# More row tiles in seven-product form, and a new layout of the last stage, in a Fourier-mixing and gated-FFN kernel

## The chip, the cores and the metric

The kernel runs on one core of one Trainium2 chip. The metric is the device time of one execution in microseconds; the times of several executions are given as a median. The profile comes from one execution of its own.

## The reference

The input `A_x` is one sequence of 2048 rows of 448 values. It is normalised row by row; from the result come a Fourier mix `s` and a gate `g`, and the output is `x + s * g`. (`B_x` isn't used.)

```python
def _A_ref(x, dft_seq_re, dft_seq_im, dft_hid_re, dft_hid_im):
    a = jnp.einsum("bsd,ed->bse", x, dft_hid_re)
    b = jnp.einsum("bsd,ed->bse", x, dft_hid_im)
    y = jnp.einsum("ts,bse->bte", dft_seq_re, a) - jnp.einsum("ts,bse->bte", dft_seq_im, b)
    return y

def _B_ref(x, w_gate, w_up, w_down):
    return (_gelu(x @ w_gate) * (x @ w_up)) @ w_down

x = A_x
xn = _layernorm(x, axis=-1)
s = _A_ref(xn, A_dft_seq_re, A_dft_seq_im, A_dft_hid_re, A_dft_hid_im)
g = _silu(_B_ref(xn, B_w_gate, B_w_up, B_w_down))
return x + s * g
```

Everything is fp32; `F` is 1792. The sequence matrices are 2048 x 2048 each.

## The kernel before

**Numbers.** TensorE works on `float32r` values. Each fp32 value is split into a high part (a rounded copy, by ACT) and a low part (the difference, by DVE), and a product is the sum of high x high, high x low and low x high, accumulated in one PSUM bank.

**Order.** All instructions stand in the order in which the program is written (`manual_schedule`, L418); each engine runs its own in that order and waits by semaphore for what it needs. SP's queue issues nearly all transfers, also in order; POOL's issues those that accumulate. A transfer on either queue carries one of eight semaphores in turn, and so also waits for the transfer eight places earlier.

**Stages.**

1. Load x, normalise, transpose, and the first feed-forward group (L419 to L615). The gate's 14 column tiles of `F` are taken in seven groups of two (`GROUPS`).
2. The other six groups (L643 to L732). Each has four blocks; a block is one call of `strassen` (L359), the gate and up products of one `F` tile for half of the rows, in a seven-product form, with four steps of the down projection (`down_one`, L318) of earlier blocks between them. `prep_s` (L231) makes sums of the next weight tiles on POOL and splits them; `load_w` and `load_d` bring them, into two halves of `raw`. Beside this, `sum_copy` and `sum_add` (L621 to L629) make sums of blocks of the sequence matrices in DRAM: a DRAM-to-DRAM copy on SP, and then a transfer on POOL's queue that adds to it. They make `sums`, 5 slots of 512 columns for each of eight passes.
3. The hidden transform (L743, `hid_mm`), for 16 row tiles k of the sequence: 22 matmuls of 448 columns each, into two of four PSUM banks. The outcome is either stored plainly, in high and low parts (`hid_plain`), or, for ten k, as seven combinations of column halves, split (`hid_seven`): a tile `TS[k]` of 128 x 3136. Six k are plain (`KP`). Of the ten, six stay in SBUF (`KR`); the four in `KX` share two tiles: all are written to DRAM (`td`) and two at a time are loaded back.
4. The last stage (L996): eight passes j, each for two row tiles t of the output (2j and 2j + 1). Per pass, each of the ten k takes seven products, `seven` (L942): 7 pairs of matmuls, high x (high, low), 448 columns, and low x high, 224 columns. That is the 2 x 2 product (two t, by the real and the imaginary part) times (real and imaginary, by two halves of the columns), in seven products for eight. The six plain k take 72 matmuls of 448 columns, `plain` (L953). Weights come from `ct` and `sums` in pieces of two k (`load_c`), get their last two sums on DVE (`combine_c`, L845), and are split (`prep_c`, L864) three units before PE uses them; a pass has 13 units. Seven PSUM banks hold the products and `gather` (L965) combines them; `give` (L980) adds the plain part and the other half, multiplies by g, adds x and stores. Two `TS` tiles are exchanged per pass, each in one transfer of 1568 KB on SP.

```python
nc.tensor.matmul(ps[q][:, :D], a, v, start=first, stop=False, skip_group_check=True)
nc.tensor.matmul(
    ps[q][:, :HD], b, v[:, :HD], start=False, stop=last, skip_group_check=True
)
```

Of the kernel before, what the change touches and what calls it, by code (L numbers as in the profile page):

```python
# [8 lines left out]
F32 = mybir.dt.float32  # L9
# [4 lines left out]
P = 128  # L14
# [16 lines left out]
KR = (0, 2, 4, 6, 9, 12)  # L31
KX = ((5, 8), (11, 14))
KP = (1, 3, 7, 10, 13, 15)
F_AT = {0: 0, 2: 0, 4: 1, 5: 0, 6: 1, 8: 0, 9: 1, 11: 0, 12: 1, 14: 1}

WHERE = "BAC"
UNITS = 13
DRAIN = {12: 2, 2: 2}


def order(j):


    q = [(t, k) for t in range(2) for k in KP]
    q = [q[i : i + 4] for i in range(0, 12, 4)]
    first = [KX[(j + 1) % 2], q[0]]
    return first[:: 1 if j else -1] + [KR[0:2], KR[2:4], KR[4:6], KX[j % 2], q[1], q[2]]

NS = 5


def slot_of(j, n):

    seven = [isinstance(what, tuple) for what in order(j)]
    return (0 if seven[n] else NS) + sum(s == seven[n] for s in seven[:n]), seven[n]
# [4 lines left out]
def fnet_geglu(ctx: ExitStack, tc: tile.TileContext, x, ct, et, wgu, wd, out):  # L62
# [20 lines left out]
    ps_mm = ctx.enter_context(tc.tile_pool(name="ps_mm", bufs=4, space=bass.MemoryType.PSUM))  # L83
    ps_tp = ctx.enter_context(tc.tile_pool(name="ps_tp", bufs=2, space=bass.MemoryType.PSUM))
    ps_o = ctx.enter_context(tc.tile_pool(name="ps_o", bufs=1, space=bass.MemoryType.PSUM))
# [6 lines left out]
    a_w = [sb.tile([P, 2560], FR, name=f"w{i}", tag=f"w{i}") for i in range(3)]  # L92
    a_d = [sb.tile([P, 1792], FR, name=f"wd{i}", tag=f"d{i}") for i in range(2)]
    a_r = sb.tile([P, 2 * 1536], F32, name="raw")
    a_t = sb.tile([P, 8 * 512], F32, name="tmp", tag="tmp")
# [16 lines left out]
    turns = [0]  # L112

    def o_tile(name, which=None):

        turns[0] += 1
        tag = which or "AB"[turns[0] % 2]
        return ps_o.tile([P, 512], F32, name=name, tag=tag)
# [44 lines left out]
    def turn_mm(c, k):  # L163
        pt = ps_tp.tile([P, 4, P], F32, name=f"pt{c}_{k}", tag="tp")
# [115 lines left out]
    def gu_ps(f, c):  # L280
        names = [f"gu{f}_{c}_{g}" for g in range(2)]
        if (f, c) == (0, 1):
            return [o_tile(n) for n in names]
        return [ps_mm.tile([P, 512], F32, name=n, tag="mm") for n in names]


    hs_of = {}

    def hs_tile(name, dt=FR):
        return sb.tile([P, 2, 512], dt, name=name, tag="hs", bufs=6)  # L290

    def new_hs(f, c):
        hs_of[f, c] = hs_tile(f"hs{f}_{c}")
        return hs_of[f, c]
# [3 lines left out]
    def act(f, c, pg):  # L298
        acts[0] += 1
        gt = tmp(acts[0] % 2)  # L300
# [17 lines left out]
    def down_one(gi, c, wdn, kk):  # L318
        if gi > 0 and kk >= 2:
            po = ps_tp.tile([P, 512], F32, name=f"po{gi}_{c}_{kk}", tag="tp")  # L320
        else:
            po = o_tile(f"po{gi}_{c}_{kk}")
# [36 lines left out]
    def strassen(f, p, w, late, dn, preps):  # L359
# [7 lines left out]
        def bank(i):  # L367
            return ps_mm.tile([P, 512], F32, name=f"x{i}_{f}_{p}", tag="mm")
# [19 lines left out]
        dn[1]()  # L388
        preps()
# [28 lines left out]
    with tc.manual_schedule():  # L418
# [11 lines left out]
        junk = hs_tile("junk")[:, 0]  # L430
# [124 lines left out]
        xf[2] = hs_tile("xf2", F32)  # L555
# [23 lines left out]
        for c in (2, 3):  # L579
# [6 lines left out]
            if c == 2:  # L586
                xf[3] = hs_tile("xf3", F32)
# [16 lines left out]
            if c == 2:  # L604
                nws[0] = prep_s(2, s_raw, nc.vector)
            else:
                nwdn = prep_d(GROUPS[1], draw)
                late_split = combine(1)
# [10 lines left out]
        sums = [dram.tile([P, NS, 512], F32, name=f"sums{j}") for j in range(NK // 2)]  # L619

        def sum_copy(j):  # L621
            src = ct[j, :NS].rearrange("n p c -> p n c")
            for q in range(2):
                nc.sync.dma_start(sums[j][:, :, 256 * q : 256 * (q + 1)], src[:, :, :256])

        def sum_add(j):
            src = ct[j, :NS].rearrange("n p c -> p n c")
            for n in (slice(0, 2), slice(2, NS)):
                nc.gpsimd.dma_start(sums[j][:, n], src[:, n, 256:768], accum_op=ALU.add)  # L629
# [13 lines left out]
        for gi in range(1, len(GROUPS)):  # L643
# [3 lines left out]
            nws, n_raw = [None, None], {}  # L647

# [34 lines left out]
            def e_split(b):  # L683

                r = n_raw["e", b]
                if b == 3:
                    e_at[b] = []
                    for i in range(2):
                        w = a_w[slots[2 if i == 0 else 0]]
                        h, q = w[:, 1792 : 1792 + D], r[:, i * D : (i + 1) * D]  # L690
# [4 lines left out]
                if b == 1:  # L695
                    v = a_d[(gi + 1) % 2]
                else:
                    v = a_w[slots[2 if b == 0 else 0]][:, :1792]
# [3 lines left out]
            for bi, (i, p, prep) in enumerate(  # L702
                ((0, 0, prep_first), (1, 0, prep_a), (0, 1, prep_d_next), (1, 1, prep_b))
            ):
                if nxt:
                    if bi == 0:
# [14 lines left out]
                at = 4 * gi + bi - 6  # L721
                if 0 <= at < NK and at % 2 == 0:
                    sum_copy(at // 2)
                elif 0 <= at < NK:
                    sum_add(at // 2)
                dn = [send] * 4
                if gi == 1 and bi < 2:
                    dn = [[nop, nop, send, send], [send, nop, send, nop]][bi]
                late = strassen(grp[i], p, ws[i], late, dn, prep)
                if i == 1:  # L730
# [5 lines left out]
        a_u = [sb.tile([P, 4096], FR, name=f"ts{p}", tag=f"u{p}") for p in range(2)]  # L736
# [3 lines left out]
        TS, ab = {}, {}  # L740
        fs = [a_r[:, : 4 * D], None]

        def hid_mm(k):  # L743
# [3 lines left out]
            for r in range(2):  # L747
                p = ps_mm.tile([P, 512], F32, name=f"ab{k}_{r}", tag="mm")
# [8 lines left out]
        def hid_plain(k, ps):  # L757
            spots = PLAIN[k]()
# [8 lines left out]
        def hid_seven(k, ps):  # L767


            f = fs[F_AT[k]].rearrange("p (i d) -> p i d", d=HD)  # L770
# [4 lines left out]
            nc.vector.tensor_sub(f[:, 4], f[:, 7], f[:, 0])  # L775
            nc.vector.tensor_sub(f[:, 3], f[:, 6], f[:, 7])
            nc.vector.tensor_sub(f[:, 5], f[:, 6], f[:, 4])
            nc.vector.tensor_sub(f[:, 1], f[:, 2], f[:, 5])
            t = SEVEN[k]()
            v = t.rearrange("p (i w d) -> p i w d", i=7, w=2)  # L780
            split(v[:, :, 0], v[:, :, 1], f[:, :7])
            TS[k] = t
            if k in td and k < NK - 2:
                nc.sync.dma_start(td[k], t.bitcast(F32))


        new = {}

        def place(name):

            if name not in new:
                if name[0] == "u":
                    new[name] = a_u[int(name[1])]
                elif name[0] == "x":
                    new[name] = a_x[int(name[1])]
                elif name == "t":
                    new[name] = sb.tile([P, 4096], FR, name="ts_t", tag="tmp")
                else:
                    new[name] = sb.tile([P, 8 * D], FR, name=f"ts_{name}", tag=name)
            return new[name]  # L800

        def seven_at(name):
            return lambda: place(name)[:, : 7 * D]

        def rest_of(*names):
            return lambda: [place(n)[:, 7 * D : 9 * D] for n in names]

        def in_hs(k):
            return lambda: [
# [297 lines left out]
```

## Time and profile before

| What | Value |
|---|---|
| Median of 3 executions | 789.19 us (788.78 to 789.21) |
| The profiled execution: its own time | 788.96 us |
| Its span, first to last instruction | 787.2 us |
| Stage 1 | 0 to 73.25 us |
| Stage 2 | 73.25 to 409.74 us |
| Stage 3 | 409.74 to 490.81 us |
| Stage 4 | 490.81 to 787.2 us |
| DMA: moved in all | 123.81 MB, mean 157 GB/s |

The profile gives busy time for TensorE's matmuls (PE), its weight loads (PEld, which overlap them), VectorE (DVE), ScalarE (ACT) and GpSimd (POOL); SPq and POOLq are the DMA queues of SyncE and GpSimd. A row of a group has line, engine, operation, what it writes and reads by name, shape and count, then busy us, mean ns of one, and the idle time just before with what ended it. In rows of DMA queues the columns are packets, MB and the time of the packets as a share of 16 engines over the stretch. In rows of transfers the last two are KB each and median us from issue to landing.

### The profile page before, as it was taken

How to read it: one execution, taken by the hardware profiler on the slowest of the kernel's cores; microseconds unless marked ns; L12 is line 12 of the kernel's file. 1: busy time of each engine (PE TensorE's matmuls, PEld its weight loads, DVE VectorE, ACT ScalarE, POOL GpSimd, SP SyncE). 2: the span in 40 equal slices, each digit the busy share in tenths (PEclk: the TensorE clock that was granted, in tenths of full speed). 3: DMA queues.
4: the chain of work that ended last, by engine and by line, in shares of the span. 5: the costliest groups of instructions: out<-in, count | busy, mean ns of one | idle time of the engine just before them, and what ended most of it. 6: DMA issues, size and time to landing. Idle time of an engine off the chain costs nothing.

```text
span 787.2 us, 10474 instructions
## 1 busy us (share of the span) xinstructions
PE 780.8 (99%) x4028; PEld 701.4 (89%) x4028; DVE 560.5 (71%) x879; ACT 297.9 (38%) x482; POOL 45.5 (6%) x64
## 2 busy tenths in 40 slices
PE   9999999999999999999999999999999999999997
PEld 7888888888888888888889999999999999999997
DVE  7877777776777677676774566776858585868676
ACT  3874442322222222232231845433434344343341
POOL 1001111031021021000000000000000000000000
PEclk9999999999999999999999999999999999999999
DMA  8001465375374383110100364959595867758590
GB/s 317 25 1 54 118 161 90 94 161 90 96 164 87 103 186 57 31 43 1 47 1 1 141 237 151 393 208 351 174 344 179 309 231 274 271 210 322 193 348 30
DMA packets 46769, 123.81 MB, mean 157 GB/s; under 512 B 3840, under 2 KB 22144, under 8 KB 43776
## 3 DMA queue, kind: packets, MB, share of 16 engines
q1 hardware_dynamic: 41344, 112.67, 40.6%
q0 software_dynamic: 5376, 10.49, 8.7%
q8 instruction: 31, 0.51, 0.3%
q14 instruction: 18, 0.15, 0.1%
HBM read 109.38 MB, written 34.73 MB: 183 GB/s over the span
## 4 chain that ended last, share of the span: by engine, by line
PE 98%; DVE 1%; issue 0%; ACT 0%
PE x L347 23%; PE po L327 17%; PE p L948 15%; PE ab L753 9%; PE p L949 7%; PE x L355 6%; PE py L961 5%; PE py L963 5%; PE py L962 5%; PE gu L278 4%; PE warm L441 1%; PE pt L166 1%; PE gu L459 1%; DVE st L134 0%; DVE xr L157 0%
## 5 line engine op out<-in xcount | busy, mean ns | idle before, releaser
L327 PE MATMUL po<-wd,hs 128*128 128x448 f32 x672 | 153.0, 366 | 0.0
L327 PEld LDWEIGHTS po<-wd,hs 128*128 128x128 f32 x672 | 125.8, 188 | 14.3
L347 PE MATMUL x<-xt,w 128*128 128x512 f32 x504 | 135.0, 391 | 0.0
L347 PEld LDWEIGHTS x<-xt,w 128*128 128x128 f32 x504 | 94.7, 188 | 16.9
L336 DVE TENSOR_TENSOR gacc<-gacc,po 128x448 f32<-128x448 f32 x96 | 59.0, 618 | 57.8 <-PE po L327 57.8
L347 PE MATMUL x<-thl,w 128*128 128x512 f32 x288 | 77.4, 391 | 0.0
L753 PE MATMUL ab<-w,xt 128*128 128x448 f32 x256 | 68.0, 365 | 0.0
L347 PEld LDWEIGHTS x<-thl,w 128*128 128x128 f32 x288 | 54.1, 188 | 10.9
L355 PE MATMUL x<-xt,w 128*128 128x512 f32 x192 | 59.2, 390 | 0.0
L398 ACT ACTIVATE hs<-tmp 128x512 fp32r<-128x512 f32 x24 | 15.2, 633 | 97.2 <-DVE tmp L396 97.2
L753 PEld LDWEIGHTS ab<-w,xt 128*128 128x128 f32 x256 | 48.1, 188 | 3.8
L387 ACT ACTIVATE tmp<-x 128x512 f32<-128x512 f32 x24 | 14.3, 597 | 88.7 <-PE x L355 88.7
L355 PEld LDWEIGHTS x<-xt,w 128*128 128x128 f32 x192 | 36.1, 188 | 7.6
L887 DVE TENSOR_TENSOR w<-raw,w 128x896 fp32r<-128x896 f32 x27 | 29.4, 1091 | 12.2 <-ACT w L886 11.3
L948 PE MATMUL p<-ts_g,xt 128*128 128x448 f32 x119 | 38.0, 374 | 0.0
L887 DVE TENSOR_TENSOR xt<-raw,xt 128x896 fp32r<-128x896 f32 x25 | 27.0, 1090 | 12.0 <-ACT xt L886 11.9
L753 PE MATMUL ab<-wd,xt 128*128 128x448 f32 x96 | 35.1, 365 | 0.0
L948 PE MATMUL p<-ts_g,w 128*128 128x448 f32 x105 | 33.5, 374 | 0.0
L278 PE MATMUL gu<-xt,w 128*128 128x512 f32 (+1 forms) x154 | 31.9, 363 | 0.0
L949 PE MATMUL p<-ts_g,xt 128*128 128x224 f32 x119 | 31.5, 265 | 0.0
L881 ACT ACTIVATE w<-raw 128x640 fp32r<-128x640 f32 x27 | 19.9, 737 | 26.3 <-PE py L962 10.9
L278 PEld LDWEIGHTS gu<-xt,w 128*128 128x128 f32 x154 | 25.8, 189 | 4.4 <-DVE xt L173 0.2
(248 smaller groups left out, 1622.2 us busy)
## 6 DMA issues: line engine op xcount, KB each, us to landing
ts_g<-td SPq DMA_DIRECT2D x16, 1568.0 KB, 10.6
sums<-ct SPq DMA_DIRECT2D x16, 640.0 KB, 6.8
raw<-ct SPq DMA_DIRECT2D x26, 384.0 KB, 4.2
raw<-ct SPq DMA_DIRECT2D x17, 512.0 KB, 8.1
raw<-wgu SPq DMA_DIRECT2D x14, 512.0 KB, 3.6
raw<-sums SPq DMA_DIRECT2D x26, 256.0 KB, 4.5
td<-ts_g SPq DMA_DIRECT2D x4, 1568.0 KB, 6.1
sums<-ct POOLq DMA_DIRECT2D x8, 768.0 KB, 7.5
```

The source lines that it names most:

```text
L278: nc.tensor.matmul(ps[:, cols], a, xt[:, k, cols], start=n == 0, stop=n == len(mm) - 1)
L327: nc.tensor.matmul(po[:, :D], hs[:, a, kk * P : (kk + 1) * P], wdn[:, b, i], start=n == 0, stop=n == 5,)
L336: nc.vector.tensor_add(ga, ga, po[:, :D])
L347: nc.tensor.matmul(ps, a[i], b[j], start=first and n == 0, stop=n == 2, skip_group_check=True)
L355: nc.tensor.matmul(ps, w["k3" + "gu"[g]][0], xt[:, 3], start=False, stop=True, skip_group_check=True)
L753: nc.tensor.matmul(p[:, :D], a, b, start=n == 0, stop=n == len(mm) - 1)
L887: nc.vector.tensor_sub(lv, src, hv)
L948: nc.tensor.matmul(ps[q][:, :D], a, v, start=first, stop=False, skip_group_check=True)
L949: nc.tensor.matmul(ps[q][:, :HD], b, v[:, :HD], start=False, stop=last, skip_group_check=True)
L961: nc.tensor.matmul(py[t][:, :D], a, vh, start=first, stop=False)
L962: nc.tensor.matmul(py[t][:, :D], a, vl, start=False, stop=False)
L963: nc.tensor.matmul(py[t][:, :D], b, vh, start=False, stop=last)
```

## The change

1. **Fourteen of the sixteen k go in seven products.** `KP` is (10, 15) alone, `KR` has ten k, `KX` four. A pass has 16 units: 14 units of one k each, and one unit for each t, with the two plain k (12 matmuls).
2. **Sums.** The host lays `ct` out as two operands of three blocks for each of the 14 k. In stage 2 `sum_step` copies one of them into `sums` and adds the other, a third of a pass's 14 k at a time (5, 5, 4): three copies on SP and three accumulating transfers on POOL for each pass, one after the other in rows of 7680 or 6144 bytes, spread over 24 blocks. Three of the seven blocks of weights are then read from `sums` and three from `ct`; the last two sums are made by one DVE step of 256 elements (`sum_c`). The plain blocks are in an array of their own, `cp`.
3. **Stage 4 laid out anew.** Weights are loaded per k, 192 KB from `ct` and 192 KB from `sums`, into five buffers of 896 columns (in `raw` and two other tiles); the split parts are in four places cut out of ends of other tiles. The seven products and the two plain banks take all eight banks, turned by one from pass to pass. The two `TS` tiles are reloaded in four pieces of 392 KB each, on SP in the first pass and on POOL's queue from the second on. x is added to the output row by an accumulating transfer on POOL, not by DVE, except in the last pass; its store follows at unit 7 or 10 of the next pass.
4. **Stage 3.** Sums and split of a tile are two steps, the split behind the next tile's sums; PSUM is used in a turn of eight banks. k = 14 is computed after 15, and its sums and split are made in the first pass of stage 4. `td` is written by POOL's queue.
5. **Stages 1 and 2.** One PSUM pool with eight named banks takes the place of three pools, with the same rotation; `hs`, the weight tiles and `xf` have other places. In the first group of stage 2 the low part of the down weights and the load behind it come later, and four down steps stand in other places.

```diff
-KR = (0, 2, 4, 6, 9, 12)
-KX = ((5, 8), (11, 14))
-KP = (1, 3, 7, 10, 13, 15)
+KR = (2, 3, 6, 7, 8, 9, 11, 12, 13, 14)
+KX = ((4, 5), (0, 1))
+KP = (10, 15)
+KS = sorted(KR + KX[0] + KX[1])
+NS = len(KS)
...
+        def sum_step(at):
+            for d in (0, 2):
+                j = (at - d) // 3
+                if (at - d) % 3 or not 0 <= j < NK // 2:
+                    continue
+                for n in (slice(0, 5), slice(5, 10), slice(10, NS)):
+                    a, b = sums[j][:, n], ct[j, d // 2, :, n]
+                    a, b = [v.rearrange("p k c -> p (k c)") for v in (a, b)]
+                    if d == 0:
+                        nc.sync.dma_start(a, b)
+                    else:
+                        nc.gpsimd.dma_start(a, b, accum_op=ALU.add)
...
+        def load_c(m):
+            v = raw_at(m)
...
+            if isinstance(k, str):
+                nc.sync.dma_start(v[:, : 4 * P], cp[2 * j + int(k[1])])
             else:
+                nc.sync.dma_start(v[:, : 3 * P], ct[j, 1, :, KS.index(k)])
+                nc.sync.dma_start(v[:, 4 * P :], sums[j][:, KS.index(k)])
+        def sum_c(m):
+            if m < len(units) and not isinstance(units[m][1], str):
+                v = raw_at(m).rearrange("p (i c) -> p i c", i=7)
+                s1 = v[:, 4:5].broadcast_to([P, 2, P])
+                nc.vector.tensor_add(v[:, 3:7:3], v[:, 1:7:5], s1)
...
+        def give(j, t):
+            c = cs[t][0]
+            def out_():
+                nc.vector.tensor_mul(c, c, gx[t])
+                nc.gpsimd.dma_start(c, xv[:, 2 * j + t, :D], accum_op=ALU.add)
+                def store():
+                    nc.sync.dma_start(ov[:, 2 * j + t], c)
+                    load_gx(j + 1, t)
+                stores.append(store)
+            return [lambda: nc.vector.tensor_add(c, c, cs[t][1]), out_]
...
+            if u < NS:
+                seven(m, k, ps, u == 0, u == NS - 1)
+                if 0 <= u - LOAD_AT < 8:
+                    i, h = divmod(u - LOAD_AT, 4)
+                    TS[KX[(j + 1) % 2][i]] = TS[KX[j % 2][i]]
+                    n, w = KX[(j + 1) % 2][i], T7 // 4
+                    part_ = slice(h * w, (h + 1) * w)
+                    eng = nc.gpsimd if j else nc.sync
+                    eng.dma_start(TS[n][:, part_].bitcast(F32), td[n][:, part_])
+            else:
+                py = bank(banks[7 if u == NS else 0], f"py{u - NS}_{j}")
+                plain(m, py)
+            if u == NS + 1 and m < len(units) - 1:
+                todo.pop()()
+            if m:
+                sum_c(m + 4)
+            if u == NS - 1:
+                todo = gather(ps)
+                for f in todo[:3]:
                     f()
+                prep_c(m + 3)
+            elif u == NS:
+                for f in todo[3:]:
+                    f()
+                prep_c(m + 3)
+                c = cs[0][0]
+                todo = [lambda c=c, py=py: nc.vector.tensor_add(c, c, py[:, :D])]
...
+            elif u == NS + 1:
+                prep_c(m + 3)
+                c = cs[1][0]
+                spare = give(j, 0)
+                spare.append(lambda c=c, py=py: nc.vector.tensor_add(c, c, py[:, :D]))
+                spare += give(j, 1)
+                banks = banks[1:] + banks[:1]
+            else:
+                if m:
+                    prep_c(m + 3)
...
+                if spare:
+                    spare.pop(0)()
+                if u in STORE_AT and stores:
+                    stores.pop(0)()
```

`prep_c(m)` splits a unit's weights and then loads unit m + 5 into the buffer that came free. `LOAD_AT` is 2, `STORE_AT` 7 and 10.

More of the change, by code (lines that the diff above doesn't have):

```diff
@@ L28, with fnet_geglu @@
 HD = D // 2
-KR = (0, 2, 4, 6, 9, 12)
-KX = ((5, 8), (11, 14))
-KP = (1, 3, 7, 10, 13, 15)
[L34 to L38, printed above, removed]
-def order(j):
[L44 to L57, printed above, removed]
+KR = (2, 3, 6, 7, 8, 9, 11, 12, 13, 14)
[3 more added lines that the diff above has]
+NS = len(KS)
+def order(j):
+    return [*KX[j % 2], *KR, *KX[(j + 1) % 2]]
 @with_exitstack
-def fnet_geglu(ctx: ExitStack, tc: tile.TileContext, x, ct, et, wgu, wd, out):
+def fnet_geglu(ctx: ExitStack, tc: tile.TileContext, x, ct, cp, et, wgu, wd, out):
     nc = tc.nc
@@ L615, in fnet_geglu @@
         late = (h1, l1)
[L619 to L629, printed above, removed]
+        sums = [dram.tile([P, NS, 3 * P], F32, name=f"sums{j}") for j in range(NK // 2)]
+        def sum_step(at):
[10 more added lines that the diff above has]
+                        nc.gpsimd.dma_start(a, b, accum_op=ALU.add)
         dq = [(0, 3, wdn, kk) for kk in range(4)]
```

472 lines of the change are left out of this document (222 added, 250 removed).

## The prediction

> **What bounds the kernel now.** I read the page's header first, then busy time by stage, then the chain of waits in the last stage.
>
> ```profile
> span 787.2 us, 10474 instructions
> PE 780.8 (99%) x4028; PEld 701.4 (89%) x4028; DVE 560.5 (71%) x879; ACT 297.9 (38%) x482; POOL 45.5 (6%) x64
> ...
> 73.25:409.74 336.49, 336.49 (x1538) 288.51 (x1537) 244.49 (x369) 99.52 (x160) 42.22 (x56) 1.00 0.39 90
> 409.74:490.81 81.07, 81.07 (x401) 75.16 (x401) 45.42 (x74) 40.59 (x51) 0.00 (x0) 1.00 0.34 128
> 490.81:527.60 36.79, 36.79 (x215) 34.72 (x215) 26.36 (x37) 16.51 (x29) 0.00 (x0) 1.00 0.77 292
> 564.20:600.80 36.60, 36.60 (x214) 34.53 (x214) 26.61 (x39) 14.42 (x24) 0.00 (x0) 1.00 0.73 260
> ```
>
> The rows under the header are stretches: length, then busy time of PE, PEld, DVE, ACT and POOL, granted clock, DMA share, GB/s. The first is the feed-forward stage (L344 to L415), the second the hidden transform (L743), the others two of the eight passes of the last stage (L996). PE is busy all of each at clock 1.00: nothing but a count of matmuls shortens these stages, and the room that the other engines have left is DVE 10 us and the DMA engines 27% in a pass of 36.6 us.
>
> ```profile
> 490.81 0.21 PE py L961
> 495.67 0.20 PE p L948
> 517.60 0.21 PE py L961
> ...
> 782.83 0.22 PE py L963
> 783.05 0.02 issue
> 784.22 0.39 DVE cc L1048
> ```
>
> From the chain (start, length, what). 490.81 to 495.67 are 24 plain matmuls: 4.86 us, 0.2027 each. 495.67 to 517.60 are ten row tiles of seven products, 70 pairs (448 columns and 224): 21.93 us, 0.3133 a pair. PE's last matmul ends at 783.05; four half-row DVE steps end at 784.61 and the last store closes the span at 787.2. The profiled execution took 788.96 us, 0.23 below the median 789.19; my sum is made against 788.96.
>
> **The change part by part.**
>
> *PE.* A pass had 70 pairs and 72 plain matmuls; it gets 98 pairs and 24 plain: 98 x 0.3133 + 4.86 = 35.56 us. Eight passes: 284.5, where 490.81 to 783.05 is 292.2 now. The first three stages keep their matmul counts. **Minus 7.7 us**, if nothing stalls. (By columns alone it would be 48 x 0.2027 = 9.7; the short matmul costs more than its columns, so I take the measured pair.)
>
> *DVE and ACT in a pass.*
>
> ```profile
> L887 DVE TENSOR_TENSOR w<-raw,w 128x896 fp32r<-128x896 f32 x27 | 29.4, 1091 | 12.2 <-ACT w L886 11.3
> L850 DVE TENSOR_TENSOR raw<-raw 128x256 f32<-128x256 f32 x26 | 10.9, 421 | 1.1 <-DMA raw<-sums 0.9
> L400 DVE TENSOR_TENSOR hs<-tmp,hs 128x512 fp32r<-128x512 f32 x24 | 17.7, 739 | 5.2 <-ACT hs L398 5.2
> L982 DVE TENSOR_TENSOR cc<-cc,py 128x448 f32<-128x448 f32 x15 | 9.2, 615 | 0.0
> L971 DVE TENSOR_TENSOR cc<-cc,p 128x448 f32<-128x448 f32 x8 | 5.0, 621 | 11.4 <-ACT cc L970 11.4
> L263 ACT ACTIVATE wd<-raw 128x896 fp32r<-128x896 f32 x7 | 6.6, 950 | 0.0
> L970 ACT ACTIVATE cc<-p 128x448 f32<-128x448 f32 x8 | 4.4, 544 | 16.4 <-PE p L949 16.4
> ```
>
> Fourteen units need a low part (1.09) and one sum of 256 elements (0.42): 21.1. Two plain units: 1.5. Seven gather steps (0.62) and six output steps (the x row is now added by a DMA): 8.1. Together 30.7 us of DVE in 35.6, 86%; ACT about 15. It is hidden on average. At the turn of a pass, from the last seven-product unit through both plain ones, DVE gets 7 x 0.62 + 0.62 + 3 x (1.09 + 0.42) = 9.5 us in PE's 2.2 + 4.9 = 7.1, and falls 2.4 us behind; the weights are prepared three units (6.6 us) ahead, so PE need not see it. The banks turn by one each pass, and the first is free after the ACT copy; I cost the turn at nothing.
>
> *The hidden transform.*
>
> ```profile
> L775 DVE TENSOR_TENSOR raw<-raw 128x224 f32<-128x224 f32 x5 | 2.0, 391 | 3.4 <-ACT raw L771 3.4
> L122 DVE TENSOR_TENSOR ts_g<-raw,ts_g 128x1568 fp32r<-128x1568 f32 x3 | 5.4, 1793 | 4.9 <-ACT ts_g L121 4.9
> ```
>
> Four more row tiles get sums and a split: 4 x 0.39 + 1.79 = 3.4 us of DVE a tile, where PE needs 22 matmuls x 0.2027 = 4.5. One fits under each; the split comes a tile later, and four banks become eight. Nothing.
>
> *Entry to the last stage.* The splits of units 1 to 3 now lie where the transform's weights were, so they wait for the last transform matmul (time T). ACT 0.95 and DVE 1.09 make unit 1 ready at T + 2.1, when PE wants it at T + 2.2. Then come unit 2's sum (0.42, to T + 2.5), its ACT copy (T + 3.5) and low part (T + 4.6); PE wants it at T + 4.6. Bounds 0 and 1.5 (the first loads into the `cc` buffer also wait for T); I take **0.3**.
>
> *The end.* Before, all but four half steps was done when PE ended (1.6 us). Now the last pass has its gather begin one pair after the last seven-product unit begins (S): PE's end is S + 2.2 + 4.9 = S + 7.1, while the other side runs the first pair and its hand-over (0.5), ACT's copy, then on DVE seven gather steps, three for one row, four for the other and four halves of 0.39: S + 0.5 + 0.54 + 14 x 0.62 + 1.6 = S + 11.3. The tail is 4.2 us instead of 1.6. Bounds 1 and 3.5 more; I take **2.6**, as each step waits for the one before.
>
> *DMA in a pass.* Packets, MB and share by queue: one whole pass (36.4 us), then 6 us with reloads (503 on), 6 us of mixed loads at full queue (497 on), 12 us in a quiet part (622 on), and 14.3 us with one pair of accumulations (90.2 on).
>
> ```profile
> q1 hardware_dynamic: 3007, 9.40, 73.8%
> ...
> q1 hardware_dynamic: 489, 2.56, 104.0%
> ...
> q1 hardware_dynamic: 982, 2.25, 97.5%
> ...
> q1 hardware_dynamic: 784, 2.04, 51.9%
> ...
> q0 software_dynamic: 672, 1.31, 59.3%
> ```
>
> The reloads give 0.039 ns per byte of one engine (104% x 6 x 16 / 2.56). Over that, a packet costs 5.9 ns at full queue (93.6 us, less 87.8 for bytes, over 982), 21 in the whole pass, 26 when quiet. An accumulated packet of 2 KB costs 202 ns. The new pass moves 14 x 2 loads of 192 KB, 2 of 256, 8 reload pieces of 392, 6 rows of 224: 10.6 MB in 5632 rows, 6336 packets with the completions (16 a transfer, as the counts before come out). Bytes 414 us, packets 37 to 165, accumulating two x rows some 25 more: **29.7 us of all 16 engines at the full-queue price, 35.7 at the whole-pass price, 37.7 at the quiet one**, in a pass of 35.6. I take the full-queue price, since the question is what a full queue can carry, and **0.5 us** in all for loads that come late.
>
> The Trainium skill, *DMA: Bandwidth & Descriptors*, section on the anatomy of one DMA (SWDGE path), fits a transfer at 2.0 us plus bytes over 436 GB/s: 2.45 us for 192 KB, four fifths of it fixed, which speaks against 28 small loads a pass. If fixed parts added up, as an estimate by that page, these loads alone would take 69 us. The trace does not agree that they do: with transfers of 224 to 384 KB among the rest, the full queue was 97.5% busy at 375 GB/s.
>
> A load is issued some three units (6.6 us) before its sum and lands in 4.2 when free (rows below), and the weights lead PE by three units.
>
> *DMA in the feed-forward stage.* The 24 pairs of copy and accumulation move 22.0 MB each instead of 10.5. By the bytes of the rows above: accumulations 22.0 x 202/2048/16 = 136 us, copies 54, and some 32 of loads now there: 222 of 336 us, instead of 131. SP sets a copy behind a weight load and the next load behind the copies; POOL's adds stand behind its accumulations.
>
> ```profile
> 111.62 0.46 POOL L240 TENSOR_TENSOR raw<-raw 128x128 f32<-128x128 f32 x1
> 117.67 1.16 ACT L242 ACTIVATE w<-raw 128x1152 fp32r<-128x1152 f32 x1
> ACT hs L398 <- DVE tmp L396: 97.2, 24, 5.0
> ...
> craw<-ct SPq DMA_DIRECT2D x1, 512.0 KB, 12.3
> ...
> raw<-ct SPq DMA_DIRECT2D x1, 512.0 KB, 3.4
> ```
>
> The tightest use, in the first group, has 5.6 us between POOL's last add and ACT's copy, and ACT then idles 4 us a block before L398. A 512 KB load that stood behind two reloads (3.2 MB) landed in 12.3 us instead of 3.4; behind the 2.75 MB of one half-row pair it would be 7.7 late. Bounds 0 and 4 us; I take **0.5**.
>
> Sum: 788.96 - 7.7 + 0.3 + 2.6 + 0.5 + 0.5 = **785.2 us**.
>
> **The rivals.**
>
> *A full DMA queue becomes the bound (slower).* If small packets keep their whole-pass or quiet price, a pass needs 35.7 to 37.7 us of DMA, and bursts leave it idle besides. DVE then waits at the sums, in order, with the low parts of the next unit behind them, and PE follows. It decides from 35.6 us per pass. One to two us in each of eight passes: 793 to 801, say **796**. For it: 3007 packets fill 73.8% now, and 6336 come. Against it: at 97.5% the overhead per packet was the smallest.
>
> *The gain is eaten by waits (no change).* Loads behind copies in the first two groups, 3 us late beyond both cushions, with the entry and the tail at their upper ends: **789**. For it: the 12.3 us landing; against it: PE waits for nothing from 73 to 410 us now.
>
> *POOL's queue lets one transfer go at a time (slower).*
>
> ```profile
> 90.23 1.32 POOL L629 DMA_DIRECT2D sums<-ct  x1 [13.07 <-DMA sums<-ct]
> 96.68 1.25 POOL L629 DMA_DIRECT2D sums<-ct  x1 [5.13 <-issue]
> POOL sums L629 <- issue: 49.7, 9, 7.4
> ...
> ts_g<-td SPq DMA_DIRECT2D x16, 1568.0 KB, 10.6
> raw<-ct SPq DMA_DIRECT2D x26, 384.0 KB, 4.2
> ```
>
> Each second accumulation left 6.45 us after the first, when that had landed. From the second pass on the reloads leave from POOL. Five of the eight pieces stand behind the x row of unit 4, so from some 5.6 units; at 4.2 each, one at a time, they end at 21 us = 9.6 units later, unit 15, and unit 13 wants the second tile: 2 units, 4.9 us, in seven passes: **819**. Against it: those accumulations had twice and three times the rows. By that page's fit (the Trainium skill, as above) a 392 KB piece takes 2.9 us; five would take 14.6 and come in time; the trace's 4.2 is the measured price.
>
> **How the numbers follow.** Forecast 0.56, full DMA 0.24, eaten gain 0.12, POOL one at a time 0.08. The likeliest alone spans 782.3 (no stall, a tail of 1) to 788. The range takes in most of the full-DMA case and leaves out the POOL case: **782.3 to 797**. A measurement of this kernel can tell 0.2%, 1.6 us, from no change. Nearly all of the forecast is faster by that; the eaten gain and a little of the others lie within; the rest is slower: 0.55, 0.15, 0.30.
>
> **What would show it.** Passes of 35.6 us with PE busy throughout show the pair price; PE idle in a pass behind ACT or DVE, those behind `raw<-sums`, with DMA shares near 1, show the full queue. PE waiting on `ts_u<-td` at units 12 and 13 shows POOL. The last PE matmul 4 us before the last DVE step shows the tail. Idle PE between 73 and 410 us shows the feed-forward waits. The prediction is wrong if the passes average over 36.3 us, or if the stages before them lose more than 3 us.

## The result, and the profile after

The changed kernel takes **797.9 us** (median; 796.36 to 802.45), the kernel before 789.16: ratio 1.0121, 95% interval 1.0078 to 1.0165. It is slower by 1.2%. The forecast was 785.2 us, in a range up to 797.0. The runs of the changed kernel also lie 6 us apart, those of before 0.4.

The page of the changed kernel, on an execution of 799.03 us: span, PE's line, DMA queues, the chain's shares by engine. Then stretches (columns as in the prediction): the feed-forward stage, three of the eight passes, the last stage as a whole, and what follows its last matmul.

```profile
span 797.3 us, 11128 instructions
PE 778.3 (98%) x4092; PEld 695.8 (87%) x4092; DVE 576.9 (72%) x933; ACT 307.0 (39%) x430; POOL 88.6 (11%) x146
...
q1 hardware_dynamic: 50144, 101.54, 36.7%
q0 software_dynamic: 10528, 54.14, 25.9%
...
PE 68%; DMA 14%; DVE 11%; issue 5%; SPq 1%; ACT 1%; DVEq 0%; ACTq 0%
```

```profile
73.00:410.00 337.00, 336.68 (x1537) 288.28 (x1536) 242.51 (x368) 99.08 (x160) 39.79 (x64) 1.00 0.59 159
...
491.10:526.80 35.70, 35.70 (x222) 33.85 (x222) 28.55 (x44) 18.91 (x22) 0.00 (x0) 1.00 0.86 295
526.80:563.10 36.30, 36.12 (x222) 33.82 (x221) 26.25 (x42) 14.74 (x17) 6.18 (x10) 1.00 0.86 285
...
675.00:713.70 38.70, 36.48 (x221) 33.80 (x221) 28.09 (x45) 15.28 (x18) 6.19 (x10) 1.00 0.85 276
...
491.10:789.30 298.20, 289.67 (x1761) 270.39 (x1760) 220.11 (x341) 120.41 (x138) 43.32 (x70) 1.00 0.85 279
789.30:797.30 8.00, 0.15 (x1) 0.00 (x0) 5.04 (x10) 0.00 (x0) 0.00 (x0) 0.64 0.16 57
```

The first pass, whose reloads leave from SP, has the forecast length and a busy PE. All the others are longer, up to 38.7 us; the PE clock is 1.00 in every pass, and the chain now runs through DMA and DVE for a quarter of the span.

What the engines waited for in the whole changed kernel (total us, times, longest), and DVE's timeline at one such place in the fifth pass (start, length):

```profile
DVE raw L889 <- DMA raw<-sums: 43.4, 25, 3.3
DVE f L889 <- DMA f<-sums: 20.8, 13, 3.5
DVE cc L997 <- DMA out<-cc: 6.3, 6, 1.8
...
PEld p L974 <- DVE xt L120: 9.1, 12, 2.0
PE p L974 <- DVE xt L120: 5.6, 10, 1.7
PEld p L973 <- DVE cc L1056: 4.5, 6, 1.2
PE p L973 <- DVE cc L1056: 2.8, 5, 1.0
```

```profile
650.65 1.08 DVE L120 TENSOR_TENSOR xt<-raw,ts_tmp 128x896 fp32r<-128x896 f32 x1
655.19 0.42 DVE L889 TENSOR_TENSOR f<-f 128x256 f32<-128x256 f32 x1 [3.45 <-DMA f<-sums]
655.53 1.08 DVE L120 TENSOR_TENSOR w<-raw,w 128x896 fp32r<-128x896 f32 x1
```

The sum of one unit (L889) waits 3.45 us for its load. The low part of the unit before it (L120, 655.53), whose data had come, stands behind that sum in DVE's order, and PE's second matmuls of the pair (L974) wait for such low parts. At the turn of a pass, PE waits for the add that frees the bank of py0 (L1056), which is late for the same reason. The two rows of weight loads (PEld) add up to 13.6 us, all of what the seven later passes lose: from gather to gather they take 37.50 us on the mean, 1.93 more than a pass without reloads (35.57, below).

The difference of the two profiled executions, 10.07 us, by parts: stages 1 to 3 end 0.31 later (491.12 for 490.81); the eight passes take 298.33 for 292.24, 6.09 more; from the last matmul (ends 789.45) to the end of the span 7.85 for 4.15, 3.70 more; outside the span 0.03 less.

### The profile page after: what moved, and what is told of

It reads as the page before. It is cut to its first block, busy times and chain, and to the rows that moved or that the text cites. A ratio compares the mean times of both kernels' runs of the same rounds, so it can differ in the third digit from the quotient of the medians.

```text
span 797.3 us, 11128 instructions
## 1 busy us (share of the span) xinstructions
PE 778.3 (98%) x4092; PEld 695.8 (87%) x4092; DVE 576.9 (72%) x933; ACT 307.0 (39%) x430; POOL 88.6 (11%) x146
## 4 chain that ended last, share of the span: by engine, by line
PE 68%; DMA 14%; DVE 11%; issue 5%; SPq 1%; ACT 1%; DVEq 0%; ACTq 0%
PE x L346 22%; PE po L326 17%; PE ab L803 9%; DMA raw<-sums 6%; PE x L354 5%; PE p L973 5%; DMA f<-sums 4%; PE gu L276 4%; DVE w L120 3%; PE p L974 2%; DVE xt L120 2%; DMA out<-cc 2%; DMA raw<-wgu 1%; DVE raw L889 1%; PE py L986 1%
## 5 line engine op out<-in xcount | busy, mean ns | idle before, releaser
L119 ACT ACTIVATE w<-raw 128x896 fp32r<-128x896 f32 (+1 forms) x61 | 54.7, 905 | 76.2 <-DVE raw L889 59.3
L889 DVE TENSOR_TENSOR raw<-raw 128x256 f32<-128x256 f32 x69 | 29.0, 420 | 43.7 <-DMA raw<-sums 43.4
L973 PE MATMUL p<-xt,w 128*128 128x448 f32 x168 | 54.5, 374 | 0.0
L119 ACT ACTIVATE w<-f 128x896 fp32r<-128x896 f32 (+1 forms) x34 | 29.9, 886 | 47.7 <-DVE f L889 35.3
L120 DVE TENSOR_TENSOR w<-raw,w 128x896 fp32r<-128x896 f32 (+1 forms) x41 | 42.8, 1045 | 2.9 <-ACT w L119 2.3
L1010 POOL DMA_DIRECT2D cc<-x x14 | 12.7, 906 | 258.7 <-DVE raw L889 196.8
L973 PE MATMUL p<-ts_u,ts_tmp 128*128 128x448 f32 x112 | 37.5, 380 | 2.9 <-DVE cc L1056 2.8
L1037 POOL DMA_DIRECT2D ts_u<-td x56 | 35.0, 755 | 12.2 <-issue 12.2
L973 PE MATMUL p<-ts_u,w 128*128 128x448 f32 x112 | 36.1, 374 | 0.0
```

What stands on the lines that cost most here:

```text
L119: nc.scalar.activation(h, src, AF.Copy)
L120: nc.vector.tensor_sub(l, src, h)
L889: nc.vector.tensor_add(v[:, 3:7:3], v[:, 1:7:5], s1)
L973: nc.tensor.matmul(ps[q][:, :D], hn, v, start=first, stop=False, skip_group_check=True)
L1037: eng.dma_start(TS[n][:, part_].bitcast(F32), td[n][:, part_])
```

## The experiments

All were timed beside the kernel before, whose medians were 788.85 to 789.07 us. "Mean pass" is worked out from one profiled execution of each: the time from the first to the last of the eight ACT copies that begin a pass's gather (L993 in the changed kernel), over seven.

| Run | What differs from the changed kernel | Median (range), us | Ratio to before (95%) | Mean pass |
|---|---|---|---|---|
| c15_changed_again | nothing | 799.76 (796.19 to 800.29) | 1.0125 (1.0103 to 1.0148) | 37.19 |
| e1_reload_sp | reloads on SP | 789.54 (787.76 to 791.61) | 1.0012 (0.9998 to 1.0025) | 36.12 |
| e2_reload_act | reloads on ACT, one a unit | 784.47 (784.35 to 786.32) | 0.9948 (0.9933 to 0.9963) | 35.84 |
| e3_no_reload | none from the second pass on | 784.16 (784.08 to 784.63) | 0.9940 (0.9925 to 0.9955) | 35.57 |
| e4_half_rows | one load a unit, longer rows (not the right weights) | 789.95 (788.11 to 791.35) | 1.0011 (1.0001 to 1.0020) | 36.43 |
| e5_bunch_act | reloads on ACT, bunched | 791.48 (788.48 to 795.41) | 1.0037 (1.0020 to 1.0055) | 36.42 |
| e18_half_pieces | reload pieces half as large | 794.04 (793.04 to 794.82) | 1.0060 (1.0043 to 1.0077) | 37.02 |

Three theories stood against each other: that the reloads come bunched and hold back the small loads (1), that the DMA engines cannot carry the traffic of a pass at all (2), and that the accumulated x rows and the stores behind them are what holds DVE (3).

**Where the reloads leave from.** e1 and e2 change one word:

```diff
-                    eng = nc.gpsimd if j else nc.sync
+                    eng = nc.sync                        (e1)
+                    eng = nc.scalar if j else nc.sync    (e2)
```

e1: 

> The eight reload pieces of each pass leave from SP between the loads of the products, one a unit, in all passes and not in the first alone. Theory 1 (the reloads come in bunches behind the two x rows on POOL and share the DMA engines with the small loads, which then land late): passes of 35.7 to 36.3 us like the first one of the changed kernel, last stage some 10 us shorter, 786 to 790 us. Theory 2 (the DMA engines can't carry 5,900 rows in 35.6 us at all): no change, 795 to 799 us. Theory 3 (the x rows added by DMA and the stores behind them hold DVE): no change, 795 to 799 us.

e2: 

> The same reload pieces leave from ACT's queue, one a unit, behind ACT's splits: spaced out, but on a queue of their own beside SP's. Theory 1, if the spacing is what counts: 786 to 790 us; if instead it counts that loads and reloads stand in one queue, 793 to 798 us with loads landing in 6 us and more. Theories 2 and 3: 795 to 799 us.

e3 keeps `eng.dma_start(...)` under `if j == 0` only. 

> From the second pass on the two tiles are not loaded again (the products there use the tiles of the pass before, so 22 MB of traffic are left out). Theory 1 and theory 2: PE is busy throughout the passes, 35.5 us each, 785 to 788 us. Theory 3: passes stay at 37 us and over, 793 to 799 us.

Stretches of e3 (without reloads) and e2 (from ACT): a fifth pass of each, and e3's last stage and tail.

```profile
633.15:668.72 35.57, 35.57 (x222) 33.82 (x221) 27.75 (x44) 15.07 (x17) 1.77 (x2) 1.00 0.71 210
490.90:775.69 284.79, 284.79 (x1761) 270.32 (x1759) 221.81 (x344) 121.74 (x138) 12.33 (x14) 1.00 0.72 213
775.69:782.40 6.71, 0.00 (x0) 0.00 (x0) 3.81 (x9) 0.00 (x0) 0.00 (x0) 0.67 0.20 68
```

```profile
634.80:670.40 35.60, 35.60 (x222) 33.85 (x221) 27.47 (x44) 15.07 (x17) 1.77 (x2) 1.00 0.91 300
777.83:784.50 6.67, 0.00 (x0) 0.00 (x0) 3.81 (x9) 0.00 (x0) 0.00 (x0) 0.76 0.20 69
```

Without reloads PE never stops, and a pass is 35.57 us. With all of them, from ACT and spread out, it is the same in four of the seven spans from gather to gather, on a profiled execution of 786.32 us, the longest of four; the kernel takes 784.47 us: 0.5% faster than before, 13.4 us faster than the change as made. So the stalls hang on the reloads, but not on their bytes alone, and e2 is the version that beats both kernels. DVE (27.75 us of 35.57) does not bind. It still waits 47.8 us for loads in all of e2 (64.2 in the changed kernel), but PE's weight loads wait only 1.4 us behind DVE, not 13.6: a late load costs time only where it uses up the lead that the weights have over PE. From SP (e1) most of the loss is gone too; what is left there is partly a wait of PE for the pieces themselves, `ts_u<-td`, 1.8 us in six places: in SP's order they leave behind loads that wait for a buffer.

**Spread or bunched, and which queue.** POOL's timeline in the fifth pass of the changed kernel, x rows and reload pieces:

```profile
645.19 0.92 POOL L1010 DMA_DIRECT2D cc<-x  x1 [26.40 <-DVE f L889]
645.79 1.96 POOL L1037 DMA_DIRECT2D ts_u<-td  x3
...
651.39 1.95 POOL L1037 DMA_DIRECT2D ts_u<-td  x3
653.99 0.55 POOL L1037 DMA_DIRECT2D ts_u<-td  x1 [0.65 <-issue]
655.59 0.55 POOL L1037 DMA_DIRECT2D ts_u<-td  x1 [1.05 <-issue]
```

The eight pieces leave within 10 us, three at a time behind each x row; in e2 they leave one by one over 18 us (637.7 to 655.4). Two 14 us stretches of a fifth pass, each where its reloads go (queues as packets, MB, share of 16 engines; transfers as KB and us to landing). The changed kernel:

```profile
q0 software_dynamic: 685, 2.49, 59.8%
q1 hardware_dynamic: 1314, 1.80, 37.6%
...
ts_u<-td POOLq DMA_DIRECT2D x8, 392.0 KB, 8.7
...
raw<-ct SPq DMA_DIRECT2D x2, 192.0 KB, 10.6
raw<-sums SPq DMA_DIRECT2D x2, 192.0 KB, 11.7
```

With reloads from ACT, spread (e2):

```profile
q1 hardware_dynamic: 1747, 2.38, 48.1%
q10 hardware_dynamic: 682, 1.90, 36.1%
q0 software_dynamic: 288, 0.46, 19.1%
...
raw<-ct SPq DMA_DIRECT2D x3, 192.0 KB, 5.0
raw<-sums SPq DMA_DIRECT2D x3, 192.0 KB, 6.1
```

The engines are full in both. In the first, POOL's queue has 60% of them and the loads (q1) 38%, and a load takes 10.6 to 11.7 us. In e3, where hardly any load is late, a sum follows the issue of its load by 5.1 to 6.7 us in most units (median 5.7), so such a load cannot be there in time. In the second the loads have 48% and land in 5 to 6.

e5 sends the pieces from ACT in bunches like POOL's:

```diff
-                if 0 <= u - LOAD_AT < 8:
-                    i, h = divmod(u - LOAD_AT, 4)
+                for piece in range(8):
+                    if u != ((4, 4, 4, 6, 6, 6, 7, 8)[piece] if j else LOAD_AT + piece):
+                        continue
+                    i, h = divmod(piece, 4)
...
+                    eng = nc.scalar if j else nc.sync
```

> Reload pieces from ACT's queue, as in the run that took 784.5 us, but three at once at unit 4, three at unit 6 and one each at units 7 and 8, which is about when POOL sent them in the changed kernel. Theory 1 (bunching): back to 793 to 799 us, with landings of the pieces near 8.6 us. Rival (POOL's software queue is what hurts, by its descriptors, whatever the moment): stays at 784 to 787 us.

791.48 us: 7.0 more than spread, so bunches cost about half of the loss without POOL. It is below the interval forecast for theory 1, and 6 to 8 us remain between it and the changed kernel. The bunches are not quite the same: in the fifth pass the second three leave 8.9 us after the first (642.44 and 651.30), not 5.6, and ACT itself is held, as issuing the first three takes it 3.80 us, and it stands idle for 3.04 us before its next split.

e4 reads each unit in one load of 3,072 byte rows from `sums`:

```diff
-                nc.sync.dma_start(v[:, : 3 * P], ct[j, 1, :, KS.index(k)])
-                nc.sync.dma_start(v[:, 4 * P :], sums[j][:, KS.index(k)])
+                n = min(KS.index(k), NS - 2)
+                nc.sync.dma_start(v[:, P : 7 * P], sums[j][:, n : n + 2].rearrange("p k c -> p (k c)"))
```

> The two loads of a product unit (128 rows of 1,536 bytes each) are one load of 128 rows of 3,072 bytes, from the sums alone, so the same bytes come with half the rows; the data and the column in which a sum is kept are others. Reloads stay on POOL. Theory 2 with a price per row of 12 ns and more: some 1,800 rows and 220 completions fewer save 1.5 us of all engines a pass, 788 to 792 us. Theory 1: the bunches remain, 793 to 797 us. Theory 3: 795 to 799 us.

These are not the weights that the products need; only the traffic is that of longer rows. 789.95 us, within theory 2's interval, and 8 us under the changed kernel with the bunches still there: half as many rows for the same bytes help too. e18 goes the other way and halves the rows of the reloads:

```diff
-                    part_ = slice(h * w, (h + 1) * w)
-                    eng.dma_start(TS[n][:, part_].bitcast(F32), td[n][:, part_])
+                    for a in (h * w, h * w + w // 2):
+                        part_ = slice(a, a + w // 2)
+                        eng.dma_start(TS[n][:, part_].bitcast(F32), td[n][:, part_])
```

> The changed kernel with its reloads in 16 pieces of 196 KB a pass, two a unit, still on POOL at the same places. On POOL a piece came as 64 packets of 6.3 KB (80 with the completions), from ACT as 128 of 3.1 KB, and the loads beside it as packets of 1.5 KB; in 10 us of a pass POOL's queue had 63% of the engines' time and the loads 38%, and these landed in 9 to 11 us. If the engines take turns between queues packet by packet, half as large packets leave the loads more: 790 to 795 us, loads landing in 6 to 8 us in the bunch. If the size of a packet doesn't matter, or the packets stay as they are: 796 to 802 us.

A 14 us stretch of the fifth pass of e18, and what PE waited for in its last stage:

```profile
q1 hardware_dynamic: 1690, 2.30, 51.3%
q0 software_dynamic: 665, 1.71, 44.2%
...
raw<-ct SPq DMA_DIRECT2D x3, 192.0 KB, 7.4
raw<-sums SPq DMA_DIRECT2D x3, 192.0 KB, 7.5
```

```profile
PEld p L973 <- DMA ts_u<-td: 6.6, 6, 1.5
PE p L973 <- DMA ts_u<-td: 6.4, 7, 1.3
```

794.04 us, as forecast for a turn by packets. A reload piece of 392 KB came from POOL in 80 packets, one of 196 KB in 64; without the 16 completions that is 6.3 and 4.2 KB a packet, a third less and not half. This stretch begins 1.9 us ahead of the first piece, that of the changed kernel 0.4 us ahead; in stretches of 14 us that all begin 0.4 us ahead, the loads have 36 to 41% in the seven passes of the changed kernel (37 to 44 in its repeat, c15) and 44 to 48% in those of e18. PE's waits for low parts are gone; of those that remain most are for the pieces, the last of which now leave later. DVE's waits for loads are 64.6 us, as many as in the changed kernel; the longest landings, as medians of one to four loads in these stretches, are 8.8 us, and 12.5 in the changed kernel.

The Trainium skill, *DMA: Bandwidth & Descriptors*, section on queues, rings and completion order, says that each engine goes round the queues that have work, a packet at a time. The shares moved the way that such a turn would move them, in e18 and, by its time, in e4; but the counts are not one for one (685 and 1314 in the changed kernel's stretch), and the profile does not show whether its packets are those of the page. The moment of the pieces changed as well in e18, so it supports that rule and does not isolate it.

**How near the engines are to full.** e10 adds DRAM-to-DRAM traffic to e2:

```diff
+                    if (u - LOAD_AT) % 2 == 0:
+                        eng.dma_start(more[j][:, (u - LOAD_AT) // 2 * w :][:, :w], td[n][:, part_])
```

> Reloads from ACT one a unit, and behind every second piece 392 KB more go from DRAM to DRAM (1.6 MB more a pass, 15%, to nowhere in use). The engines' share was 0.87 of the time in the passes without it. If only bunches hurt and the engines have room for 15% more: 784 to 787 us. If 0.87 was already near what small loads with a lead of three units stand: 790 to 800 us. At a full bound of 35.2 us of DMA a pass nothing would have to be lost.

810.66 us (808.94 to 812.14), ratio 1.0280 (1.0262 to 1.0299), 26 us over e2 and beyond the 790 to 800 us of the second case. One of its passes:

```profile
609.05:648.10 39.05, 36.67 (x221) 33.69 (x220) 27.43 (x44) 14.82 (x17) 1.73 (x2) 1.00 0.93 314
```

0.93 x 39.05 is 36.3 us of engines for a pass, where e2 has 0.91 x 35.60 = 32.4. The share of a whole pass does not go beyond 0.93: cut into stretches of 2.6 us, it is 0.92 to 1.08 through most of this pass, and 0.74 in the first and 0.62 and 0.29 in the last two, where few transfers are under way. As far as this one added stream tells, e2 is within a few per cent of what a pass can hold: theory 2 is right about the room and wrong about the traffic as it is, which fits when it is spread.

**The x rows.** e6 is e2, and e11 the changed kernel, both without `nc.gpsimd.dma_start(c, xv[...], accum_op=ALU.add)` in `give`.

e6: 

> Reloads from ACT one a unit, and the x row of all but the last two row tiles is not added (14 rows of 224 KB less, and no wait of DVE's store for it). If the accumulated x rows are what is left of the stalls at the turn of the pass (four PE waits on the py0 add, some 1.3 us of PE idle): 782.5 to 784 us. If they cost nothing: 784 to 785 us.

784.45 us (784.38 to 784.59): they cost nothing where the pieces are spread.

e11: 

> The changed kernel without the accumulated x rows in 14 of 16 row tiles. POOL then has nothing ahead of the reload pieces, and all eight leave at once after units 0 and 1, some 2 units earlier, in a tighter bunch. Theory 1: still stalls, 788 to 798 us. Theory 3 (x rows and the stores behind them are what costs): 784 to 786 us.

793.21 us (791.99 to 796.27): theory 1; seven pieces left at once, 2 us after the start of the pass. Theory 3 falls. But when the engines are full, the x rows do count. e9, e12, e13 and e14 put a POOL copy of one column ahead of each piece, to spread them on POOL:

```diff
+                    if j:
+                        nc.gpsimd.tensor_copy(gate, c_hl[m + 2][1][:, :1].bitcast(F32))
                     eng.dma_start(TS[n][:, part_].bitcast(F32), td[n][:, part_])
```

e9: 

> Reload pieces on POOL as in the changed kernel, but ahead of each, from the second pass on, POOL reads one column of the low part that DVE made one unit earlier, so that at most one piece leaves a unit. Theory 1 (bunching alone): 784 to 787 us, as from ACT. Rival (POOL's software queue costs some 6 us by itself, the difference between the changed kernel and bunches from ACT): 789 to 793 us.

e12 (also without x): 

> Reload pieces on POOL, each behind POOL's read of one column of the low part made one unit earlier, and the x row of 14 of 16 row tiles is not added, so that nothing else holds POOL. If the pieces then leave over some 18 us of a pass (from 3 to 21 us after its start, as from ACT) and spreading is what counts: 784 to 786 us, as from ACT without x (784.45). If POOL's software queue costs by itself, however spread: 789 to 793 us. If they leave within 12 us all the same, the run tells nothing apart.

e13 (`[0]` for `[1]` in the gate): 

> As the run before (POOL, no x in 14 row tiles), but POOL reads a column of the high part, which ACT makes, not of the low part. That is what ACT's own pieces stand behind, so they should leave from 3 to 20 us after the start of a pass. Spreading alone counts: 784 to 786 us. POOL's software queue costs by itself: 788 to 793 us.

e14 (e13 with x): 

> The same with the x rows kept: they stand in POOL's order ahead of the first and of the fourth piece and wait for DVE. If an x row's wait is what holds the pieces back and bunches them: pieces from 6 us on, 790 to 798 us, although each has its gate. If the x rows hold nothing: as the run without them.

797.30, 788.70, 788.66 and 797.05 us. POOL's timeline in e13, fifth pass:

```profile
643.38 5.46 POOL L1038 COPY gate<-w 128x1 f32<-128x1 f32 x1
648.78 0.55 POOL L1039 DMA_DIRECT2D ts_u<-td  x1
...
655.12 0.55 POOL L1039 DMA_DIRECT2D ts_u<-td  x1
```

The pieces begin late (the first leaves at 642.84), and seven of them leave within 6.3 us (648.78 to 655.12), and much the same behind the other gate; so these runs did not spread them and do not tell POOL's queue from the bunch. What they show is the price of the x rows beside such bunches: 8.4 us between e14 and e13, whose pieces leave over 12 to 13 us alike, 4.7 between the changed kernel and e11, nothing between e2 and e6.

**What else was tried.** e16 stores finished rows from ACT (`nc.scalar.dma_start(ov[:, 2 * j + t], c)`), to take away the 6.3 us in which the gather waits for the store of the row before. 

> The changed kernel with its finished rows stored from ACT's queue, not SP's, where the store stands behind loads that wait for DVE to free a buffer; reloads stay on POOL. In the changed kernel DVE waits 5 to 6 us in six turns of the pass for that store. If this wait is what lies between it and the bunches from ACT (791.5 us): 791 to 794 us and no wait of the gather for out. If it only stands where a load would otherwise be waited for: 796 to 801 us.

799.25 us (798.19 to 802.70): the wait for `out<-cc` is gone, and DVE's waits for loads have grown from 64.2 to 72.1 us (46.0 and 26.1; the profiled execution took 802.70 us, 3.7 more than that of the changed kernel). The wait had only stood in their place.

e17 sends all eight pieces from ACT at unit 2, without x (e5's edit with 2 for the list of units). 

> From the second pass on all eight reload pieces leave from ACT at unit 2, and the x row of 14 of 16 row tiles is not added: the same burst, some 2 to 7 us after the start of a pass, as in the run from POOL without x (793.2 us). Only the queue differs. If the burst alone costs: 791 to 795 us. If POOL's queue costs by itself: 785 to 789 us.

812.58 us (806.87 to 814.09), outside both: ACT itself was held. Its timeline:

```profile
645.87 9.23 ACTq L1037 DMA_DIRECT2D ts_u<-td  x8
655.20 1.79 ACT L119 ACTIVATE w<-f 128x896 fp32r<-128x896 f32 x2 [8.46 <-DMA ts_u<-td]
```

Eight transfers took 9.23 us to issue, and the splits stood behind them. So the run says nothing of POOL's queue.

e7 is e2 with a real layout of 3,072 byte rows: copies of six blocks, accumulations onto three of them.

```diff
-                    a, b = sums[j][:, n], ct[j, d // 2, :, n]
+                        nc.sync.dma_start(sums[j][:, n], ct[j, :, n])
...
+                        for o in range(n.start, n.stop, 3):
+                            q = slice(o, min(o + 3, n.stop))
+                            nc.gpsimd.dma_start(sums[j][:, q, 3 * P :], ca[j, :, q], accum_op=ALU.add)
```

> Reloads from ACT one a unit, and each product unit in one load of 3,072 byte rows: the copies of stage 2 write six blocks of a tile, not three (11 MB more read and written there), and the accumulations reach three of them, in 40 transfers, not 24. If rows still cost something once the reloads are spread: the passes lose their last 1.3 us, 782.5 to 784 us, provided that the longer copies delay no weight load; if those do, PE idles between 73 and 410 us and the whole takes 785 to 790 us.

857.58 us (853.69 to 866.00), a miss. What POOL and PE waited for in e7:

```profile
POOL sums L638 <- issue: 322.6, 44, 22.8
...
PE x L346 <- DVE tmp L398: 64.3, 4, 24.1
```

The accumulations (48 transfers, not the 40 of the expectation) show 13,696 packets between 73 and 480 us, where the changed kernel has 3,456 in all. They hold POOL's queue, POOL's adds of weights stand behind them (ACT waits 78.7 us for these, DVE 78.2 for ACT), and PE loses 64 us in the feed-forward stage. Its passes are 35.57 us all the same.

e8 is e2 with the last two adds of x as `nc.gpsimd.tensor_add`. 

> Reloads from ACT one a unit, and the x of the last two row tiles is added by POOL, not DVE. After the last matmul DVE then has 11 steps of its chain left over, not 13: if the chain of DVE alone sets the end, 1.2 us less, 783 to 783.6 us; if POOL's adds take over 1.5 us each and the last pair waits for them, no gain, 784 to 785.5 us.

784.83 us (784.33 to 785.86), no gain. The tail of e8:

```profile
776.19 1.14 POOL L1063 TENSOR_TENSOR cc<-cc,f 128x448 f32<-128x448 f32 x1 [22.04 <-DVE cc L1062]
776.67 1.14 DVE L1065 TENSOR_TENSOR cc<-cc 128x448 f32<-128x448 f32 x1
...
778.55 1.13 POOL L1067 TENSOR_TENSOR cc<-cc,raw 128x448 f32<-128x448 f32 x1 [1.22 <-DVE cc L1066]
778.87 1.05 DVE L1071 TENSOR_TENSOR cc<-cc,f 128x224 f32<-128x224 f32 x1
```

The DVE add beside POOL's takes 1.14 us, not 0.62, and the half one 1.05, not 0.39: what the two steps saved is lost there.

c15, the control: 

> The changed kernel itself, beside the two: 796 to 802 us, as before.

799.76 us (796.19 to 800.29), as expected.

## Why the prediction was wrong

By its own steps:

- **PE, minus 7.7: right.** Without stalls eight passes take 284.79 us (e3), forecast 284.5. The price of the pair, read from the ten-tile pass, held.
- **Stages 2 and 3 and the entry, plus 0.8 in two terms: nearly right.** Measured 0.31; PE idles 0.32 us between 73 and 410 us, with 24 pairs of long transfers there. e7 shows that this cover has an end.
- **The tail, plus 2.6: right.** 6.67 to 6.71 us after the last matmul in e2 and e3, 4.15 before: 2.5 more. In the changed kernel it was 3.70; in its last gather DVE waits 1.0 us for the store of the row before (L997).
- **The turn of the pass and DVE: right that they cost nothing by themselves.** I summed 30.7 us of DVE; it is busy 27.75 (e3), as the records of steps in a row overlap by some 0.08 us and I added whole lengths. PE's wait for the py0 add appears only where loads are late.
- **DMA in a pass, 29.7 us, and "0.5 us in all for loads that come late": the step that failed.** The price was 2.7 us low (32.4 in e2), and that is not what broke it. I set a mean for a pass against the length of a pass, found it smaller, and concluded that loads would come in time. But a load has a median of 5.7 us from issue to sum (I took 6.6), and the reload pieces leave POOL within some 10 us. In that stretch the engines are full, the loads get 38% of them, and they land in up to 11.7 us. Measured: the passes take 298.33 us, not 284.5 + 0.5, **13.3 us** more, and average 37.3 us, over the 36.3 that I named as a sign of being wrong. The sign was in sight: I had the landing of 12.3 us behind two reloads on the page, and used it for stage 2 alone; and in the very stretch that gave the full-queue price (497 to 503 us) loads of 384 and 512 KB landed in 6.4 and 8.7 us.
- **The full-DMA rival** named the chain that came (DVE at the sums, low parts behind them, PE) and its size (1 to 2 us a pass, 796; measured 1.9 on the mean of the seven later passes). Its point of decision, 35.6 us of engines a pass, was too high: the share of a pass never went over 0.93, and loads were late already at some 32 us when reloads were bunched.
- **POOL one at a time: did not come.** POOL's waits ahead of the reloads are 12.2 us in 15 places, 1.5 at most, and PE never waits for `ts_u` in the changed kernel. But POOL's place in the story was real: behind the x rows its pieces leave late and together.

With the DMA step mended by spreading, the sum holds, term by term and not by luck: e2's 784.47 beside 785.2.

What stays open: why bunches cost 6 to 8 us more from POOL than from ACT. Turns by packets (80 packets for a piece from POOL, 144 from ACT) would do it, and e18 and e4 speak for that; but the bunches from ACT (e5) also lay further apart, and that may be part of it. No run has the pieces spread on POOL.

## What to carry to other kernels

Compare DMA demand with capacity over the time that a load has from issue to use, not over a whole pass: a mean share of 0.86 hides a stretch in which small loads get 38% of the engines. Spread large transfers that are not urgent between the urgent small ones, one at a time, from a queue whose order paces them; and look at what stands ahead of them there, since a transfer that waits for data lets everything behind it go at once. Give an engine that both computes and issues one transfer at a time: here eight at once held it 9.23 us, three 3.80.

## What the runs showed of the hardware

- ACT was held 9.23 us by issuing eight transfers of 392 KB at one place (e17), by issuing three 3.80 us (e5), by one a unit 0.33 to 0.37 us each (e2).
- A DVE add of two SBUF operands beside a POOL add took 1.14 us instead of 0.62 (e8). The Trainium skill, *SBUF — State Buffer*, section on the two separate sides, says that the port pair shared by the two engines is locked for a whole instruction, and that a DVE operation with two SBUF inputs wants it against a GpSimd one that reads SBUF; the trace agrees, as both DVE adds began while POOL's ran and ended 0.48 and 0.24 us after it, a little less than their own 0.62 and 0.39.
- A transfer of 392 KB came in 80 packets from POOL and 144 from ACT. With pieces half as large, which also left over a longer time, the loads' share of the engines rose from 36 to 41% to 44 to 48% (e18).
